# Halved VectorE conversions, two more PSUM banks and later clears in a windowed attention followed by two MLPs

## The chip, the cores and the metric

The kernel runs on one core of a Trainium2 chip. The metric is the time of one execution in microseconds (us) of device time, as the median of several runs. One further execution was recorded by the hardware profiler; all rows below come from it.

## The reference

```python
# attention: B, H, S, D = 4, 8, 576, 64; key j counts for query i where 0 <= i - j < 128
scores = scale * np.matmul(q, k.transpose(0, 1, 3, 2))
scores = np.where(mask, scores + bias[None], -1000000000.0)
attn = softmax(scores);  x = (attn @ v) as 2304 tokens x 512
# first MLP: w_in 512 x 2048, w_out 2048 x 512
h = x @ w_in
g = np.where(h >= 1, h, np.where(h <= -1, 0.0, (h + 1) ** 2 / 4))
x = g @ w_out
# second MLP, weights of the same sizes
h = x @ w_in2
out = (h * np.clip(h + 3.0, 0.0, 6.0) / 6.0) @ w_out2
```

The weights of both MLPs arrive as 64-bit floats. All products are done to nearly 32-bit accuracy, by splitting each operand into a high and a low part.

## The kernel before

The program has three stretches that matter here.

**The opening.** The tokens are cut into units (64 to 256 queries of one batch), and a step is one block of 128 queries (or fewer) of one head of a unit. `Attention.tick` issues one step's stages: `stage_a` multiplies a query block with its keys into a PSUM bank (tile `s`, L418), VectorE adds the table of distances and takes the row's extreme (L448, tiles `p` and `sm`), ScalarE takes the exponential (L452). Two ticks later `stage_b` transposes the result on TensorE (tile `t`, L476 and L477), and ScalarE copies it to `tt`. Three ticks later `stage_c_whole` multiplies it with the values (tile `r`, L514), and at the end of a pair of heads VectorE divides (`rec`, L526 and L527, and `y`, L528). `stage_d_whole` transposes `y` (tile `x` in PSUM, L539), and ScalarE and VectorE write it as a high and a low part into the large tile `x` that feeds the first MLP (L151, L158). The opening runs 37 ticks: the 32 steps of units 0 and 1, and the first steps of unit 2. While `u.unit < 2` the scores take three PSUM banks in turn (`s`, `acc0`, `acc1`) and the transposes two (`t`, `t2`); from unit 2 on they take one each.

**The first block of the first MLP.** `run_block` goes over the 16 pieces f of 128 hidden units for the first 512 tokens. `Mlp.first` makes the first product of piece f, twelve matrix products of 512 columns into one bank (tile `h`, L671). `Mlp1.activate` makes g of it on VectorE, ScalarE and GpSimd: for even f L711, L712, L713, for odd f L704, L705, L706, then the split into a high part (ScalarE, L151) and a low part (GpSimd, L158). Only with L713 or L706 done is the bank free. `Mlp.second` multiplies the g of two pieces earlier into four accumulators (tile `acc`, L724, twelve products). The banks of h are the tags in `mlp1.tags`, here `("h0",)`: one bank, so that the first product of piece f + 1 waits for the activation of piece f. The accumulators are the banks `acc0`, `acc1`, `h1`, `t2`, taken when the first second product is issued, after the first product of piece 2. The remaining ticks of units 2 and 3 are spread through this block.

**The conversion of the first MLP's weights** runs through both. For each piece f, `conv1` makes on ScalarE the shifted magnitude `ma` (L194) and an integer (L198) of the raw words `rawa`, and on GpSimd the sign (L197); `conv2` joins them on VectorE, a shift with or (L205) and an integer addition (L212); `conv3` splits the result into a high part (ScalarE, L151) and a low part (VectorE, L158), tile `wa`. Each handles [128, 1024] elements: the piece's columns of w_in and rows of w_out, 512 each. Pieces 0 to 2 are begun in the opening, at the ticks of `CONV_AT`; the others inside the first block, the conversion of piece f + 2 being finished after the first product of piece f.

`Attention.clear` zeroes at the program's start the half of each of the eight key buffers `kw` that the zero padding needs (L312, VectorE).

A scheduler lays out the instructions of TensorE, VectorE, ScalarE and GpSimd in this part, engine by engine, from the order of the code and its own estimates; each engine then works its list strictly in order. Only SyncE, which issues the transfers, follows the code's own order. After the first block the other blocks of the first MLP (256 and 384 tokens, with the rest of the attention between) and then the second MLP follow, to about 948 us.

Of the kernel before, what the change touches and what calls it, by code (L numbers as in the profile page):

```python
# [9 lines left out]
F32 = mybir.dt.float32  # L10
# [3 lines left out]
I32 = mybir.dt.int32  # L14
# [28 lines left out]
def tile_window_attention_two_mlps(  # L43
# [118 lines left out]
    class Weights:  # L162
# [37 lines left out]
        def conv2(self, f):  # L200


            raw, m = self.raw[f], self.m[f]
            if self.sign_pool:
                nc.vector.scalar_tensor_tensor(out=m.bitcast(U32), in0=m.bitcast(U32), scalar=3, in1=raw[..., 1],  # L205
                                               op0=ALU.logical_shift_left, op1=ALU.bitwise_or)
            else:
                nc.vector.tensor_scalar(out=m.bitcast(U32), in0=m.bitcast(U32), scalar1=3, scalar2=None,
                                        op0=ALU.logical_shift_left)
                nc.vector.scalar_tensor_tensor(out=m.bitcast(U32), in0=raw[..., 1], scalar=0x80000000,  # L210
                                               in1=m.bitcast(U32), op0=ALU.bitwise_and, op1=ALU.bitwise_or)
            nc.vector.tensor_tensor(out=m.bitcast(I32), in0=m.bitcast(I32), in1=raw.bitcast(I32)[..., 0], op=ALU.add)  # L212

        def conv3(self, f):
            del self.raw[f]
            m = self.m.pop(f)
            hl = wpool.tile([P, 2, 2, PIECE], F32R, tag=f"w{f}", name=f"w{self.nm}{f}")
            split_hi("act", hl[:, 0], m)
            split_lo("dve", hl[:, 1], m, hl[:, 0])
            self.hl[f] = hl  # L220

        def conv_part(self, part):
# [54 lines left out]
    class Attention:  # L277
        def __init__(self, raw, proc, work, xs):
            self.raw, self.proc, self.work, self.xs = raw, proc, work, xs
            self.n_load = self.n_prep = self.t = 0  # L280
            self.row, self.low, self.sum, self.late = None, None, None, []
            self.k_owners, self.v_owners = [], []

            self.vts = [raw.tile([P, KCH, 2 * D + 2], F32, tag="vr", name=f"vr{i}", bufs=3) for i in range(3)]

            kr = [raw.tile([P, 2, KMAX], F32, tag="kr", name=f"kw{i}") for i in range(2)]
            qr = [raw.tile([P, 2, UMAX], F32, tag="qr", name=f"qw{i}") for i in range(2)]
            self.kw = [t[:, j] for t in kr for j in range(2)]
            self.kw += [proc.tile([P, KMAX], F32, tag=tag, name=f"kw_{tag}{i}") for tag in ("kh", "kl") for i in range(2)]
            self.qw = [t[:, j] for t in qr for j in range(2)]  # L290
            self.pt = [work.tile([P, 2 * P], F32, tag="p", name=f"p{i}", bufs=LAG_B + 1) for i in range(LAG_B + 1)]
            a = next(h for h in range(H) if plain not in (h, h + 1))
            self.pt.append(dist[:, a:a + 2].bitcast(F32).rearrange("p a b -> p (a b)"))
            free = [h for h in range(a + 2, H) if h != plain]
            self.tc = [dist[:, h:h + 2].bitcast(F32R).rearrange("p a (s q) -> p a s q", s=1)[:, :, 0] for h in free[:4:2]]
            assert len(self.tc) == 2 and all(h + 1 in free for h in free[:4:2])
            self.near, self.takes = zeros[:, :P], zeros[:, P:]
            self.n_p = self.n_tc = 0
# [6 lines left out]
            nc.gpsimd.affine_select(out=self.takes, in_=self.takes, compare_op=ALU.is_ge, fill=0.0,  # L305
                                    base=0, pattern=[[-1, P]], channel_multiplier=1)

        def clear(self):

            for i, k in enumerate(self.kw):  # L310
                a = D * (1 - i % 2)
                nc.vector.memset(k[a:a + D, :], 0.0)  # L312

        def load_whole(self, n):

# [105 lines left out]
        def stage_a(self, n, i):  # L421
# [5 lines left out]
            qo, ko = a - u.q0, ks - u.k0  # L427
            bo = 0 if a >= P else P

            tag = ("s", "acc0", "acc1")[(n * 2 + i) % 3] if u.unit < 2 else "s"  # L430
            ps = psum.tile([P, BANK], F32, tag=tag, name=f"s{n}_{i}")
            u.n_a += 1
            if u.unit == 0:
# [27 lines left out]
        def stage_b(self, n, i):  # L461
# [4 lines left out]
            if i == 0:  # L466
                u.tt = self.work.tile([P, 2, 2 * QB, P], F32 if u.whole else F32R, tag="tt", name=f"tt{n}")
            pt = u.p.pop(i)
            bank = psum.tile([P, BANK], F32, tag=("t", "t2")[(n * 2 + i) % 2] if u.unit < 2 else "t",
                             name=f"t{n}_{i}")  # L470
            ps = bank.rearrange("p (s q) -> p s q", q=P)

# [381 lines left out]
    with ExitStack() as actx:  # L854
# [6 lines left out]
        att = Attention(raw, proc, work, XX)  # L861

        nc.vector.memset(zeros, 0.0)
        att.clear()

        nc.scalar.copy(minus_odd, nc.const_aps.tensor(0.0, [P, 1], F32))
        bank = psum.tile([P, BANK], F32, tag="h1", name="busy")
# [6 lines left out]

        for t in range(unit_steps[0] + unit_steps[1] + LAG_D + 1):
            att.tick()
            if t in LOAD_AT:
                W1.load()
            if t in CONV_AT:
                with att.behind(), att.behind_exp():  # L880
                    W1.conv_part(CONV_AT[t])

        def spread(ticks):

            slots, att0 = 2 * KF, att.t

            def hook(f, after):
                k = 2 * f + after + 1
                W1.load()
                with att.behind(), att.behind_exp():  # L890
                    for part in ((2,) if after else (3, 1)):
                        W1.conv_part(part)
                while att.t < att0 + min(ticks, -(-ticks * k // (slots - 2))):
                    att.tick()

            return hook
# [14 lines left out]

            return hook

        mlp1.tags = ("h0",)
        ticks = unit_steps[2] + unit_steps[3]
        att.make_tables()
        run_block(mlp1, 0, FULL, spread(ticks))
# [434 lines left out]
```

## Time and profile before

| | us |
|---|---|
| median of 3 runs (948.9 to 949.98) | 949.7 |
| the profiled execution | 950.16 |
| its span, first to last instruction | 948.4 |
| TensorE busy (matrix products) | 931.3 |
| VectorE busy | 652.2 |
| ScalarE busy | 535.2 |
| GpSimd busy | 297.1 |

In the profile PE is TensorE's products, PEld its weight loads, DVE VectorE, ACT ScalarE, POOL GpSimd, SP SyncE. A busy time is a union of spans, and the end of a product is modelled, so that a busy PE can still hide short gaps. The duration of an instruction reaches past the start of the next one; how long an engine is taken is the distance from start to start. PEclk is the granted TensorE clock as a share of 2.4 GHz. "[0.52 <-ACT tt L151]" behind a row is idle time ahead of it and the instruction that ended it.

### The profile page before, as it was taken

What the parts mean: (1) busy time and instruction counts of PE and PEld (TensorE: products, weight loads), DVE (VectorE), ACT (ScalarE), POOL (GpSimd) and SP (SyncE); (2) the same over time, 40 slices, a digit from 0 to 9 for tenths busy, and PEclk for the clock granted to TensorE, in tenths of its full rate; (3) what the DMA queues carried; (4) which work ended last, traced back from release to release, by engine and by line L of the source; (5) the groups of instructions that cost most, each with busy time, mean ns of one, the idle gap of its engine ahead of it and who ended that gap; (6) DMA issues with size and microseconds to landing.
All of it is one profiled execution on the core that took longest, in us unless ns stands there. A gap on an engine that the chain in (4) does not pass through costs nothing.

```text
span 948.4 us, 16369 instructions
## 1 busy us (share of the span) xinstructions
PE 931.3 (98%) x5299; PEld 855.1 (90%) x5299; DVE 652.2 (69%) x1706; ACT 535.2 (56%) x1325; POOL 297.1 (31%) x559
## 2 busy tenths in 40 slices
PE   9999999999999999999999999999999999999998
PEld 7777878999999999999999999999998898988887
DVE  5778786786777676766745899958557777644443
ACT  6877876676666666666634886635343334322233
POOL 2133555797668676767720000000000000000000
PEclk9999999999999999999999999999999999999999
DMA  6665512222213222221007862005264644543431
GB/s 195 207 207 193 179 48 73 82 82 84 69 52 88 63 60 63 73 90 48 15 27 250 281 230 90 1 18 172 78 211 157 239 167 151 168 125 117 122 112 66
DMA packets 92644, 112.74 MB, mean 119 GB/s; under 512 B 8720, under 2 KB 70416, under 8 KB 92560
## 3 DMA queue, kind: packets, MB, share of 16 engines
q1 hardware_dynamic: 92560, 111.71, 36.8%
q8 instruction: 42, 0.69, 0.3%
q14 instruction: 42, 0.34, 0.1%
HBM read 87.56 MB, written 24.12 MB: 118 GB/s over the span
## 4 chain that ended last, share of the span: by engine, by line
PE 73%; DVE 7%; ACT 3%; issue 2%; POOL 1%; DMA 1%; SPq 0%; ACTq 0%; POOLq 0%; DVEq 0%
PE acc L777 21%; PE h L671 21%; PE acc L724 13%; PE y L1253 7%; PE x L1253 5%; PE r L562 2%; PE s L418 2%; PE t L477 1%; DVE kl L398 1%; DVE x L158 1%; DVE r L711 1%; DVE r L713 1%; DVE ma L212 1%; DMA x2r<-x2d 1%; ACT r L712 0%
## 5 line engine op out<-in xcount | busy, mean ns | idle before, releaser
L671 PE MATMUL h<-x,wa 128*128 128x384 f32 (+2 forms) x1152 | 222.7, 340 | 4.3 <-DVE r L713 3.1
L777 PE MATMUL acc<-wb,g 128*128 128x512 f32 x861 | 222.2, 393 | 0.0
L724 PE MATMUL acc<-g,wa 128*128 128x384 f32 (+2 forms) x1152 | 222.1, 339 | 0.0
L671 PEld LDWEIGHTS h<-x,wa 128*128 128x128 f32 x1152 | 192.1, 189 | 16.0 <-DVE r L713 6.8
L724 PEld LDWEIGHTS acc<-g,wa 128*128 128x128 f32 x1152 | 190.9, 188 | 5.9
L777 PEld LDWEIGHTS acc<-wb,g 128*128 128x128 f32 x861 | 159.4, 188 | 24.9
L151 ACT CAST g<-r 128x384 fp32r<-128x384 f32 (+2 forms) x192 | 98.2, 511 | 71.0 <-DVE r L1200 37.5
L158 POOL TENSOR_TENSOR g<-r,g 128x384 fp32r<-128x384 f32 (+2 forms) x80 | 87.4, 1093 | 55.9 <-ACT g L151 46.1
L158 DVE TENSOR_TENSOR g<-r,g 128x384 fp32r<-128x384 f32 x112 | 62.3, 556 | 41.9 <-ACT g L151 41.4
L712 ACT ACTIVATE r<-r 128x384 f32<-128x384 f32 (+2 forms) x88 | 45.1, 514 | 70.5 <-DVE r L711 70.3
L495 POOL TENSOR_SCALAR_AFFINE_SELECT tt<-dist 128x256 fp32r<-128x256 f32 (+1 forms) x176 | 77.7, 461 | 16.1 <-DVE dist L490 15.7
L711 DVE TENSOR_SCALAR r<-h 128x384 f32<-128x384 f32 (+2 forms) x88 | 47.5, 540 | 40.5 <-PE h L671 32.0
L671 PE MATMUL h<-x,wb 128*128 128x384 f32 x384 | 72.6, 336 | 0.0
L452 ACT ACTIVATE p<-p,sm 128x128 f32<-128x128 f32 (+2 forms) x134 | 57.4, 430 | 24.8 <-DVE sm L448 24.5
L671 PEld LDWEIGHTS h<-x,wb 128*128 128x128 f32 x384 | 68.2, 188 | 2.6
L713 DVE TENSOR_TENSOR r<-h,r 128x384 f32<-128x384 f32 (+2 forms) x88 | 47.8, 544 | 23.7 <-ACT r L712 21.8
L1198 ACT ACTIVATE r<-u 128x384 f32<-128x384 f32 x32 | 16.8, 525 | 56.2 <-DVE u L1262 56.2
L562 PEld LDWEIGHTS r<-tt,vs 128*128 128x128 f32 x304 | 45.1, 189 | 3.4 <-POOL tt L495 1.3
L400 POOL TENSOR_TENSOR qs<-qr,qs 128x256 fp32r<-128x256 f32 (+2 forms) x64 | 39.0, 610 | 27.1 <-ACT qs L397 15.1
L562 PE MATMUL r<-tt,vs 128*128 128x128 f32 (+3 forms) x304 | 44.8, 262 | 1.6 <-POOL tt L495 0.9
L398 DVE SCALAR_TENSOR_TENSOR kl<-kr,kh 128x256 fp32r<-128x256 f32 (+3 forms) x64 | 39.2, 612 | 0.0
L477 PE MATMUL t<-ident,p 128*128 128x128 f32 x134 | 38.2, 289 | 0.7 <-DVE x L158 0.6
(169 smaller groups left out, 1567.4 us busy)
## 6 DMA issues: line engine op xcount, KB each, us to landing
w<-wd SPq DMA_DIRECT2D x88, 256.0 KB, 2.7
rawa<-w_in SPq DMA_DIRECT2D x16, 512.0 KB, 4.5
rawa<-w_out SPq DMA_DIRECT2D x16, 512.0 KB, 5.6
rawb<-w_in SPq DMA_DIRECT2D x16, 512.0 KB, 4.0
rawb<-w_out SPq DMA_DIRECT2D x16, 512.0 KB, 4.9
wd<-sum SPq DMA_DIRECT2D x32, 256.0 KB, 2.1
wd<-wb SPq DMA_DIRECT2D x24, 256.0 KB, 2.8
out<-o SPq DMA_DIRECT2D x17, 256.0 KB, 2.4
```

The source lines that it names most:

```text
L151: nc.scalar.copy(hi, x)
L158: engines[eng].tensor_tensor(out=lo, in0=x, in1=hi.bitcast(F32), op=ALU.subtract)
L398: nc.vector.scalar_tensor_tensor(out=u.kl[:, :nk], in0=u.kr[:, :nk], scalar=unit, in1=u.kh[:, :nk].bitcast(F32), op0=ALU.mult, op1=ALU.sub ...
L452: self.exp = nc.scalar.activation(out=pt[:, :nk], in_=pt[:, :nk], func=AF.Exp, bias=sm[:, 0:1], scale=-1.0, accum_out=None if u.whole else ...
L495: nc.gpsimd.affine_select(out=u.tt[:, :, s0 + s, :m], in_=both, compare_op=ALU.is_ge, fill=0.0, base=-1 + s, pattern=[[0, 2], [sign, m]], ...
L562: nc.tensor.matmul(u.r[:, qo:qo + nq], u.vs[:, j, c, :, :].rearrange("p a d -> p (a d)"), u.tt[:, part].rearrange("p s q -> p (s q)")[:, s ...
L671: nc.tensor.matmul(ps[:, :n], self.W.w_in(a, c, f), self.x_chunk(x, b, c, n), start=(k == 0), stop=(k == 3 * KC - 1))
L711: nc.vector.tensor_scalar(out=r[:, :n], in0=ps[:, :n], scalar1=-1.0, scalar2=1.0, op0=ALU.max, op1=ALU.min)
L713: self.larger = nc.vector.tensor_tensor(out=r[:, :n], in0=ps[:, :n], in1=r[:, :n], op=ALU.max)
L724: nc.tensor.matmul(acc[i][:, o * n:(o + 1) * n], self.W.w_out(a, f)[:, e * P:(e + 1) * P], g[:, b, :n], start=(first and k == 0 and o == 0 ...
L777: nc.tensor.matmul(acc[t][:, :DM], g[:, b, tg * P:(tg + 1) * P], self.W.w_out(a, f), start=(first and k == 0), stop=(last and k == 2))
L1253: nc.tensor.matmul(ps[:, :N2], w[:, a, c * P:(c + 1) * P], self.x.operand(k, c, b), start=(start and n == 0), stop=(n == 5), skip_group_ch ...
```

## The change

The two `conv2` operations and the low part of `conv3` are issued on VectorE in two halves of 512 columns (`self.sign_pool` is set for the first MLP's weights alone), the shift and the addition of one half before those of the other. The first product of piece 1 takes the bank `t2` instead of `h0`: `mlp1.tags` is `("h0", "t2")` until piece 1, then `("h0",)`. The three banks of scores and the two of transposes stay in use to the end of the opening (`self.open`), so also for the first steps of unit 2. Four of the eight key buffers are cleared at the start, two behind the first tick and two behind the second.

```diff
@@ conv2
             if self.sign_pool:
-                nc.vector.scalar_tensor_tensor(out=m.bitcast(U32), in0=m.bitcast(U32), scalar=3, in1=raw[..., 1],
-                                               op0=ALU.logical_shift_left, op1=ALU.bitwise_or)
+                for k in range(2):
+                    nc.vector.scalar_tensor_tensor(out=m.bitcast(U32)[:, k], in0=m.bitcast(U32)[:, k], scalar=3,
+                                                   in1=raw[:, k, :, 1], op0=ALU.logical_shift_left, op1=ALU.bitwise_or)
+                    nc.vector.tensor_tensor(out=m.bitcast(I32)[:, k], in0=m.bitcast(I32)[:, k],
+                                            in1=raw.bitcast(I32)[:, k, :, 0], op=ALU.add)
+                return
...
@@ conv3
             split_hi("act", hl[:, 0], m)
-            split_lo("dve", hl[:, 1], m, hl[:, 0])
+            if self.sign_pool:
+                for k in range(2):
+                    split_lo("dve", hl[:, 1, k], m[:, k], hl[:, 0, k])
+            else:
+                split_lo("dve", hl[:, 1], m, hl[:, 0])
@@ Attention
+            self.open = True
...
-        def clear(self):
-
-            for i, k in enumerate(self.kw):
+        def clear(self, places):
+
+            for i in places:
                 a = D * (1 - i % 2)
-                nc.vector.memset(k[a:a + D, :], 0.0)
+                nc.vector.memset(self.kw[i][a:a + D, :], 0.0)
...
-            tag = ("s", "acc0", "acc1")[(n * 2 + i) % 3] if u.unit < 2 else "s"
+            tag = ("s", "acc0", "acc1")[(n * 2 + i) % 3] if self.open else "s"
...
-            bank = psum.tile([P, BANK], F32, tag=("t", "t2")[(n * 2 + i) % 2] if u.unit < 2 else "t",
+            bank = psum.tile([P, BANK], F32, tag=("t", "t2")[(n * 2 + i) % 2] if self.open else "t",
@@ the opening and the first block
-        att.clear()
+        att.clear(range(4))
...
             att.tick()
+            if t < 2:
+                with att.behind():
+                    att.clear(range(4 + 2 * t, 6 + 2 * t))
...
                 W1.load()
+                if f == 1:
+                    mlp1.tags = ("h0",)
...
-        mlp1.tags = ("h0",)
+        mlp1.tags = ("h0", "t2")
+        att.open = False
```

TensorE's list where the opening goes over into the first block; `h` is the first product, `wa_469` and then `wa_471` hold piece 0's weights, `wa_616` and then `wa_621` piece 1's, and `x_742`, then `x_750`, is the transpose of the last pair of heads of unit 1. Before:

```order
L514 MATMUL r_724<-vr_105,tt_727 128x65 x2
L476 MATMUL t_0_755<-ident,p_115 128x128
L477 MATMUL t_0_755<-ident,p_115 128x128
L418 MATMUL s_0_764<-kw_kh_110,qw_109 128x192
L476 MATMUL t_0_806<-ident,p_116 128x128
L477 MATMUL t_0_806<-ident,p_116 128x128
L539 MATMUL x_742<-ident,y_704 128x128 x2
L671 MATMUL h<-x,wa_469 128x512 x12
```

And of the changed kernel, in the same place:

```order
L679 MATMUL h<-x,wa_621 128x512 x2
L522 MATMUL r_730<-vr_105,tt_714 128x65 x2
L484 MATMUL t_0_734<-ident,p_114 128x128
L485 MATMUL t_0_734<-ident,p_114 128x128
L679 MATMUL h<-x,wa_621 128x512 x3
L522 MATMUL r_730<-vr_105,tt_733 128x65 x2
L484 MATMUL t_0_763<-ident,p_115 128x128
L485 MATMUL t_0_763<-ident,p_115 128x128
L547 MATMUL x_750<-ident,y_710 128x128 x2
L426 MATMUL s_0_772<-kw_kh_110,qw_109 128x192
L679 MATMUL h<-x,wa_471 128x512 x12
```

Five of the twelve first products of piece 1 now stand ahead of piece 0's, between the opening's last transposes; piece 0's twelve stand ahead of one transpose that they stood behind. Seven products of piece 1 follow piece 0's, and then those of piece 2, ahead of the first second product; before, the twelve of piece 2 stood within the second products of piece 0.

VectorE's list around the division for that last pair of heads (`rec_703`, then `rec_709`, and `y_704`, then `y_710`), with piece 2's `conv2` in it. Before:

```order
L526 TENSOR_SCALAR rec_703<-r_654 128x4
L205 SCALAR_TENSOR_TENSOR ma_667<-ma_667,rawa_449 128x1024
L527 RECIPROCAL rec_703<-rec_703 128x4
L212 ISA ma_667<-rawa_449,ma_667 128x2048
L528 TENSOR_TENSOR y_704<-r_654,rec_703 128x256
```

And of the changed kernel:

```order
L534 TENSOR_SCALAR rec_709<-r_660 128x4
L206 SCALAR_TENSOR_TENSOR ma_673<-ma_673,rawa_451 128x512
L535 RECIPROCAL rec_709<-rec_709 128x4
L206 SCALAR_TENSOR_TENSOR ma_673<-ma_673,rawa_451 128x512
L536 TENSOR_TENSOR y_710<-r_660,rec_709 128x256
L208 ISA ma_673<-rawa_451,ma_673 128x1024 x2
```

Between `rec` and `y` there were a whole shift and a whole addition; now there are the two halves of the shift, and the addition stands behind `y`.

VectorE's list at the program's start, as one piece of the difference:

```order
-L312 MEMSET kw_kh_110 64x384
-L312 MEMSET kw_kh_111 64x384
-L312 MEMSET kw_kl_112 64x384
-L312 MEMSET kw_kl_113 64x384
 L128 TENSOR_SCALAR odd<-odd 128x1
...
+L320 MEMSET kw_kh_110 64x384
+L456 ISA p_115,sm_1_185<-s_1_182,dist 128x256
+L456 ISA sm_1_185 128x1
+L320 MEMSET kw_kl_112 64x384
+L320 MEMSET kw_kh_111 64x384
+L320 MEMSET kw_kl_113 64x384
+L456 ISA p_116,sm_0_197<-s_0_194,dist 128x128
```

One of the four later clears now stands behind the first step's row operation and three behind the second's, ahead of the third's.

## Rows read from the trace of the kernel before

**Rows 1.** Busy time by stage: us, then PE, PEld, DVE, ACT, POOL, clock, DMA.

```profile
0.00:50.49 50.49, 46.39 (x302) 36.91 (x303) 33.62 (x127) 36.11 (x88) 9.76 (x32) 1.00 0.67 200
50.49:62.26 11.77, 10.33 (x50) 8.40 (x49) 7.30 (x17) 7.88 (x15) 3.02 (x4) 0.86 0.91 288
62.26:110.00 47.74, 46.63 (x243) 38.64 (x243) 38.50 (x67) 38.39 (x65) 19.82 (x22) 1.00 0.48 160
110.00:160.00 50.00, 47.79 (x233) 37.77 (x232) 39.17 (x82) 37.03 (x74) 29.63 (x30) 1.00 0.31 94
```

**Rows 2.** PE in order of time: start, us, instruction, count, idle ahead.

```profile
48.68 0.66 PE L514 MATMUL r<-vr,tt 128*128 128x65 f32 x4 [0.52 <-ACT tt L151]
...
50.35 0.38 PE L539 MATMUL x<-ident,y 128*128 128x128 f32 x2
50.49 2.99 PE L671 MATMUL h<-x,wa 128*128 128x512 f32 x12
...
56.77 2.65 PE L671 MATMUL h<-x,wa 128*128 128x512 f32 x6 [1.44 <-DVE r L713]
...
73.19 2.91 PE L671 MATMUL h<-x,wa 128*128 128x512 f32 x12
75.93 0.27 PE L477 MATMUL t<-ident,p 128*128 128x128 f32 x1
```

**Rows 3.** VectorE in order of time, from 47 to 57 us.

```profile
47.20 0.16 DVE L526 TENSOR_SCALAR rec<-r 128x4 f32<-128x4 f32 x1
47.30 1.22 DVE L205 SCALAR_TENSOR_TENSOR ma<-ma,rawa 128x1024 uint32<-128x1024 uint32 x1
48.45 0.17 DVE L527 RECIPROCAL rec<-rec 128x4 f32<-128x4 f32 x1
48.56 1.22 DVE L212 CUSTOM_DVE_ANT_0 ma<-rawa,ma 128x2048 uint16<-128x2048 uint16 x1
49.70 0.42 DVE L528 TENSOR_TENSOR y<-r,rec 128x256 f32<-128x256 f32 x1
...
53.72 0.68 DVE L711 TENSOR_SCALAR r<-h 128x512 f32<-128x512 f32 x1
...
56.02 0.69 DVE L713 TENSOR_TENSOR r<-h,r 128x512 f32<-128x512 f32 x1
```

**Rows 4.** PE's waits, 44 to 160 us: us in total, times, longest.

```profile
PE s L418 <- DVE sm L448: 1.5, 3, 0.6
PE h L671 <- DVE r L713: 1.4, 1, 1.4
```

**Rows 5.** The program's first steps in order of time, PE and VectorE.

```profile
3.94 0.77 PE L418 MATMUL s<-kw,qw 128*128 128x128 f32 x2
...
4.23 0.87 DVE L312 MEMSET kw_kl<- 64x384 f32 x2
...
5.39 0.29 DVE L448 CUSTOM_DVE_ANT_0 p<-s,dist 128x128 f32<-128x128 f32 x1
...
6.37 0.29 DVE L448 CUSTOM_DVE_ANT_0 p<-s,dist 128x128 f32<-128x128 f32 x1
```

**Rows 6.** VectorE, an operation of 256 columns and the start of the next.

```profile
30.51 0.42 DVE L158 TENSOR_TENSOR x<-x,x 128x256 fp32r<-128x256 f32 x1
30.85 0.41 DVE L448 CUSTOM_DVE_ANT_0 p<-s,dist 128x256 f32<-128x256 f32 x1
```

**Rows 7.** GpSimd and VectorE side by side, 121 to 126 us.

```profile
121.54 1.95 POOL L158 TENSOR_TENSOR g<-r,g 128x512 fp32r<-128x512 f32 x1 [0.47 <-ACT g L151]
123.45 2.13 POOL L197 TENSOR_SCALAR rawa<-rawa 128x1024 f32<-128x1024 f32 x1
...
122.51 2.06 DVE L212 CUSTOM_DVE_ANT_0 ma<-rawa,ma 128x2048 uint16<-128x2048 uint16 x1
```

**Rows 8.** The last piece: its conversion's end on VectorE, its first product.

```profile
149.78 1.22 DVE L158 TENSOR_TENSOR wa<-ma,wa 128x1024 fp32r<-128x1024 f32 x1
...
156.52 2.88 PE L671 MATMUL h<-x,wa 128*128 128x512 f32 x12
```

More of the change, by code (lines that the diff above doesn't have):

```diff
@@ L204, in conv2 @@
             if self.sign_pool:
-                nc.vector.scalar_tensor_tensor(out=m.bitcast(U32), in0=m.bitcast(U32), scalar=3, in1=raw[..., 1],
-                                               op0=ALU.logical_shift_left, op1=ALU.bitwise_or)
[L207 to L211, printed above, removed]
+                for k in range(2):
[4 more added lines that the diff above has]
+                return
+            nc.vector.tensor_scalar(out=m.bitcast(U32), in0=m.bitcast(U32), scalar1=3, scalar2=None,
+                                    op0=ALU.logical_shift_left)
+            nc.vector.scalar_tensor_tensor(out=m.bitcast(U32), in0=raw[..., 1], scalar=0x80000000,
+                                           in1=m.bitcast(U32), op0=ALU.bitwise_and, op1=ALU.bitwise_or)
             nc.vector.tensor_tensor(out=m.bitcast(I32), in0=m.bitcast(I32), in1=raw.bitcast(I32)[..., 0], op=ALU.add)
```

## The prediction

> **What bounds the kernel now.** I first read the busy time by stage [rows 1]. From 62 to 160 us TensorE is busy 94.4 of 97.7 us at full clock, while VectorE is busy 77.7 of them (79%) and ScalarE 75.4 (77%): TensorE carries the first block, and the others get in its way for 3.3 us in all. Behind 160 us the change touches nothing but times of arrival, and TensorE's list goes on in the same order, so a us that TensorE is ahead at the end of the first block should be a us at the end of the program. The two stretches ahead of it are looser. In the opening TensorE shows 4.1 us of idle time, and more is hidden in chains from step to step. Between 50.5 and 62.3 us it is idle for 1.44 us and runs at a granted clock of 0.86.
>
> Then I read TensorE in order of time at that seam [rows 2], and who it waited for [rows 4]. The reader is to see one wait: the first product of piece 1 starts at 56.77 us because its only bank is held until piece 0's L713, which starts at 56.02 us [rows 3]. It is the longest wait of the block, and behind it the clock falls to the lower of its two levels (1.2 GHz). A mean of 0.86 over 11.77 us [rows 1] costs 0.14 × 11.77 = 1.65 us.
>
> **The change, part by part.**
>
> *The bank for piece 1.* With its own bank, piece 1's first product follows piece 0's at once: the 1.44 us of waiting go, and with the idle time gone the 1.65 us of lower clock should go too, 3.1 us in all. What is late next is piece 2, which needs piece 0's bank. Ahead of it TensorE has seven products of piece 1: twelve take 75.93 - 73.19 = 2.74 us [rows 2], 0.228 each, so seven take 1.6 us. From the end of piece 0's product the bank needs L711 (0.6 of a row of 0.68, whose tail overlaps the next), two halves of `conv3` that now stand behind it (1.2, below) and L713 (0.7), 2.5 us, with ScalarE's part beneath the halves. So the new wait is between nothing and 0.9 us; four short attention products also lie ahead, and I take 0.5. The term is 3.1 - 0.5 = 2.6 us; its bounds are 0.5 (the clock still falls, and the wait is 0.9) and 3.1.
>
> *The five products moved ahead.* They stand between the transposes of the opening's last steps, where TensorE waited for ScalarE, as for 0.52 us at 48.68 [rows 2]. They are worth 5 × 0.228 = 1.14 us where they fit wholly into waits, and nothing where they push the transposes back. More of that place is idle than the marked wait, so I take 1.0.
>
> *The division ahead of the seam.* Piece 0's product waits for the transpose of `y` (50.35 us), that for `y` (49.70), and that stood behind a whole shift and a whole addition, from 47.30 on [rows 3]. An operation of 1024 columns takes 1.15 us from start to start [rows 3], one of 256 takes 0.34 [rows 6]: 1.06 ns a column and 0.067 us fixed, so a half takes 0.61. Two halves of the shift remain ahead of `y`, so it comes 1.1 us earlier. But TensorE's own steps ahead of that transpose, paced by ScalarE, end barely half a us sooner than they did. Bounds 0 and 1.1; I take 0.7, nearer to the upper since one transpose has left their front.
>
> *The banks for unit 2.* The wait of scores for VectorE's row operation is 1.5 us in three places, the longest 0.6 [rows 4], and only that first place is in the opening. Bounds 0 and 0.6; I take 0.2, because the next steps are paced by ScalarE.
>
> *The clears.* A clear takes 0.44 us (two in 0.87) [rows 5]. The first row operation started at 5.39 us, behind all eight, though its product was finished by 4.71: up to 0.6 us. The third step's row operation, at 6.37, now has three clears ahead: up to 1.3 us lost there. Between these I take a gain of 0.3, as the steps behind it wait for more than VectorE.
>
> The sum ahead of the first second product is 2.6 + 1.0 + 0.7 + 0.2 + 0.3 = 4.8 us.
>
> *The halves inside the first block.* Three more operations for each of 16 pieces at 0.067 us are 3.2 us more of VectorE, some 2.7 of them in the block. VectorE has 20 us of idle time there [rows 1], so the cost isn't felt directly; but TensorE's 3.3 us of waits come where VectorE is late with a row operation or an activation. Halves also change who waits for GpSimd. At 121.54 a GpSimd operation was running, VectorE's addition came at 122.51 and ended at 124.57, 2.06 us for one that takes 1.14 to 1.22 [rows 3, 7]; GpSimd's next came at 123.45 and ended 1.0 us after that addition. They took turns whole. A half that meets a GpSimd operation waits as long as a whole did, and there are twice as many. With some 5 us of such waits beside the 2.7, VectorE's idle time falls from 20 to 13 us, and if waits grow as idle time shrinks, 3.3 become 5.1: 1.8 us. Against that, a row operation now waits 0.6 us instead of 1.15 where the list puts it between halves. I take 1.5 us of loss; bounds are a gain of 3.3 (all waits gone) and a loss of more than the 4.8.
>
> The last piece's weights are ready at about 151 us and used at 156.5 [rows 8]: 5.5 us of slack, just more than the lead. So a lead up to that size needs no faster conversion.
>
> The Trainium skill, "SBUF — State Buffer", Who interferes with whom, says that a VectorE operation with two SBUF inputs and a GpSimd operation that reads SBUF lock each other out for a whole instruction. Rows 7 agree, with 2.06 us against 1.14. By that rule each boundary between halves is a place for GpSimd to step in, which is the slower rival below.
>
> Net, 4.8 - 1.5 = 3.3 us. The profiled execution took 950.16 us (span 948.4 and 1.8 around it), so it would take 946.9; it lies 0.46 above the median of 949.7, on which the forecast is **946.4 us**.
>
> **The rivals.**
>
> *Given back.* VectorE, ScalarE and GpSimd run the first block at nearly their own pace, since each works its list in order, and TensorE, arriving 4.8 us early, waits for them bit by bit until it is where it was. For it: both VectorE and ScalarE are near 80% busy. Against it: the slack of the last piece, and idle time on all three. It gives 949.7 less 0 to 1.9 us.
>
> *Slower, by turns with GpSimd.* Each piece has two long GpSimd operations, L197 and the low part of g. If both come in at a boundary between two halves, VectorE waits 2 × 0.95 us more for a piece (2.06 less about 1.1) [rows 7], 25 us over 13 pieces, with the 2.7 more than its 20 us of idle time: VectorE becomes the bound. It decides when the added waits pass 17 us. The block then grows by 25 + 2.7 - 20 = 7.4 us, less 4.8: 952.3 us. Against it: in most places a whole operation already followed a whole one, so GpSimd could step in there too.
>
> *More is gained.* The smaller operations also take away most of the 3.3 us of later waits instead of adding to them: 4.8 + 2.5 = 7.3 us, 942.4. What speaks for it is 21% of idle time on VectorE; what speaks against it is that the lists mostly put the two halves back to back. The Trainium skill, "Perfetto Trace Analysis", Optimizing Scalar/DVE Operations, says that where these engines aren't saturated but make others wait, breaking up instructions may let work finish sooner. With VectorE at 79% that rule's condition holds here, and by it this case would be the outcome.
>
> **How the numbers follow.** The likeliest case has 0.55, with its own range 943.9 to 947.8 (a net gain of 1.9 to 5.8 us, inside the terms' bounds); given back 0.2; slower by turns 0.13; more is gained 0.12. Differences of 0.2% (1.9 us) are about what a measurement of this kernel can tell from no change. Faster by more than that: 0.55 + 0.12 = 0.67. Within it: 0.2. Slower: 0.13. The range that leaves out 2 in 10 runs from 942.0, which takes in most of the larger gain, to 950.2, which takes in what is given back but not the slower case.
>
> **What would show it.** In the changed profile the first product of piece 0 should start near 49 us instead of 50.49, with five products of piece 1 ahead of it. No wait of 1.4 us should follow it, only one of about 0.5 ahead of piece 2, and the granted clock should stay at 1.00 between 50 and 70 us. The first second product should start near 60 us with 36 first products behind it, instead of 24 at 62.26. A half should take about 0.6 us from start to start. TensorE's waits from there to the last piece should be near 5 us. The prediction is wrong if the clock falls at another place of the seam, if VectorE passes 90% in the first block, or if TensorE's lead at the last piece is far from its lead at the first second product.

## The result, and the profile after

The changed kernel takes 955.71 us (median of 4 runs, 954.2 to 956.2) against 949.84 (948.9 to 950.48). The ratio is 1.0063, with a 95% interval of 1.0048 to 1.0078: it is slower, where the forecast was 946.4 us. The profiled execution has a span of 953.7 us against 948.4.

Busy time by stage after the change, cut at the first product of piece 1 in its new place, at the first second product (62.75 us) and at the first product of block 1 (167.99); columns as in [rows 1]:

```profile
0.00:48.83 48.83, 44.89 (x293) 37.28 (x293) 32.05 (x130) 35.52 (x86) 9.48 (x30) 0.97 0.66 199
48.83:62.75 13.92, 12.50 (x68) 10.06 (x67) 11.18 (x28) 8.53 (x17) 3.42 (x7) 0.99 0.68 219
...
62.75:167.99 105.24, 95.79 (x472) 75.72 (x471) 89.58 (x183) 76.40 (x140) 49.77 (x51) 1.00 0.39 127
```

The stretch of the kernel before from its first second product to the first product of block 1:

```profile
62.26:161.96 99.70, 96.37 (x481) 78.02 (x481) 78.36 (x149) 76.52 (x140) 49.45 (x51) 1.00 0.40 127
```

Two things are to be seen. At its first second product the changed kernel is ahead. It comes 0.49 us later, but behind 36 first products instead of 24, and twelve of them are 2.74 us [rows 2], so the lead is 2.25 us. At block 1's first product it is 167.99 - 161.96 = 6.03 us behind. So 8.3 us were lost between the two, inside the first block. There TensorE is idle for 9.45 us instead of 3.33, and VectorE is busy for 89.58 instead of 78.36. ScalarE and GpSimd do the same work in the same time.

VectorE's conversions from 50 to 170 us, grouped (count, then busy us, mean ns of one, idle time ahead). Before:

```profile
L212 DVE CUSTOM_DVE_ANT_0 ma<-rawa,ma 128x2048 uint16<-128x2048 uint16 x13 | 20.8, 1599 | 0.1
L158 DVE TENSOR_TENSOR wa<-ma,wa 128x1024 fp32r<-128x1024 f32 x14 | 17.3, 1236 | 11.2 <-ACT wa L151 11.1
L205 DVE SCALAR_TENSOR_TENSOR ma<-ma,rawa 128x1024 uint32<-128x1024 uint32 x13 | 17.0, 1305 | 4.8 <-POOL rawa L197 4.7
```

After:

```profile
L208 DVE CUSTOM_DVE_ANT_0 ma<-rawa,ma 128x1024 uint16<-128x1024 uint16 x27 | 28.0, 1060 | 0.0
L158 DVE TENSOR_TENSOR wa<-ma,wa 128x512 fp32r<-128x512 f32 x28 | 22.5, 836 | 0.8 <-ACT wa L151 0.7
L206 DVE SCALAR_TENSOR_TENSOR ma<-ma,rawa 128x512 uint32<-128x512 uint32 x26 | 20.8, 827 | 6.8 <-POOL rawa L197 6.8
```

The same columns are converted in 71.3 us instead of 55.1 (sums of the three groups). Where the 16 us are is seen in the changed kernel in order of time, 87 to 92 us, all engines:

```profile
87.13 1.27 DVE L158 TENSOR_TENSOR wa<-ma,wa 128x512 fp32r<-128x512 f32 x2
...
88.30 1.30 POOL L158 TENSOR_TENSOR g<-r,g 128x512 fp32r<-128x512 f32 x1 [4.85 <-ACT g L151]
...
88.47 3.20 DVE L208 CUSTOM_DVE_ANT_0 ma<-rawa,ma 128x1024 uint16<-128x1024 uint16 x2
...
89.74 1.40 POOL L197 TENSOR_SCALAR rawa<-rawa 128x1024 f32<-128x1024 f32 x1
...
91.59 0.34 DVE L456 CUSTOM_DVE_ANT_0 p<-s,dist 128x192 f32<-128x192 f32 x1
91.76 1.05 ACT L151 CAST wa<-ma 128x1024 fp32r<-128x1024 f32 x1 [1.95 <-DVE ma L208]
...
92.00 0.49 PE L426 MATMUL s<-kw,qw 128*128 128x128 f32 x2 [1.07 <-DVE sm L456]
```

A pair of halves (of the low part) with GpSimd idle for most of it takes 1.27 us (87.13). The pair at 88.47 (of the addition) takes 3.20: it runs beside one GpSimd operation, and a second one begins within it. The row operation behind it comes late, ScalarE waits 1.95 us for the addition, and TensorE 1.07 us for the row operation. It is one of many: of the 81 halves in 50 to 170 us, 18 take over 0.5 us more than the shortest of their kind, none more than 1.14, and each of the 18 overlaps a GpSimd operation that reads. In the kernel before it is 6 of 40 whole operations.

TensorE's waits from 62 to 167 us after the change (us in total, times, longest), as in [rows 4]:

```profile
PE s L426 <- DVE sm L456: 4.0, 6, 1.1
...
PE h L679 <- DVE r L714: 1.7, 2, 1.1
...
PE t L485 <- DVE x L158: 1.6, 2, 0.8
...
PE r L522 <- ACT tt L151: 1.2, 2, 1.0
```

Nearly all of them end with VectorE. None is long; there are simply more of them (15, against 6 in the kernel before from 62 to 162 us).

At the seam, TensorE in order of time after the change (compare [rows 2]):

```profile
45.21 0.66 PE L522 MATMUL r<-vr,tt 128*128 128x65 f32 x4 [1.51 <-ACT tt L151]
...
46.80 1.20 PE L679 MATMUL h<-x,wa 128*128 128x512 f32 x2
47.80 0.95 PE L522 MATMUL r<-vr,tt 128*128 128x65 f32 x4
...
50.83 3.06 PE L679 MATMUL h<-x,wa 128*128 128x512 f32 x12
...
54.53 1.91 PE L679 MATMUL h<-x,wa 128*128 128x512 f32 x7
...
57.41 0.51 PE L679 MATMUL h<-x,wa 128*128 128x512 f32 x1 [0.97 <-DVE r L721]
```

The bank wait of 1.44 us is gone. In its place are 0.97 us ahead of piece 2, and a new wait of 1.51 us for ScalarE at 45.21, behind which the products of 46.80 and 47.80 run slowly: the granted clock is 0.83 from 40 to 50 us, and 1.00 from 50 to 70.

### The profile page after: what moved, and what is told of

It is laid out like the page before. It is cut to its first block, busy times and chain, and to the rows that moved or that the text cites. A ratio compares the mean times of both kernels' runs of the same rounds, so it can differ in the third digit from the quotient of the medians.

```text
span 953.7 us, 16417 instructions
## 1 busy us (share of the span) xinstructions
PE 931.1 (98%) x5299; PEld 855.1 (90%) x5299; DVE 665.6 (70%) x1754; ACT 534.9 (56%) x1325; POOL 297.4 (31%) x559
## 4 chain that ended last, share of the span: by engine, by line
PE 78%; DVE 10%; ACT 5%; issue 3%; POOL 2%; DMA 1%; SPq 0%; ACTq 0%; POOLq 0%; DVEq 0%
PE h L679 22%; PE acc L785 21%; PE acc L732 14%; PE y L1267 7%; PE x L1267 5%; PE s L426 3%; PE r L570 3%; DVE ma L208 2%; PE t L485 2%; DVE ma L206 1%; DVE kl L406 1%; PE r L522 1%; DVE wa L158 1%; DVE r L719 1%; DVE x L158 1%
## 5 line engine op out<-in xcount | busy, mean ns | idle before, releaser
L151 ACT CAST g<-r 128x384 fp32r<-128x384 f32 (+2 forms) x192 | 98.1, 511 | 67.6 <-DVE r L1214 37.6
```

What stands on the lines that cost most here:

```text
L151: nc.scalar.copy(hi, x)
```

## The experiments

Each experiment was timed in five rounds beside the kernel before on its own chip (medians of 949.8 to 950.0 us). Theory A says that the halves cost, because VectorE's two-input operations (both inputs in SBUF) and GpSimd's take turns and more boundaries let GpSimd in. Theory B puts the loss on the seam and the clock's fall there, and theory C on the number of operations and their places in VectorE's list. Besides the times, two measures stand in the table: the conversions' time (sum of the three groups, 50 to 170 us), and the length of the first block, from the first second product to block 1's first product, which starts behind 36 first products, or behind 24 where the table says so.

| kernel | us | conversions, us | first block, us |
|---|---|---|---|
| before | 949.84 | 55.1 | 99.70 (24) |
| after | 955.71 | 71.3 | 105.24 |
| halves_only | 960.77 | 71.4 | 108.37 (24) |
| whole_rest | 947.64 | 57.5 | 98.23 |
| hbank_only | 947.79 | 57.3 | 98.15 |
| open_only | 951.52 | 56.6 | 99.36 (24) |
| hbank_clears | 946.78 | 57.2 | 98.23 |
| before_memset | 947.19 | 55.0 | 98.16 (24) |
| after_memset | 949.02 | 66.6 | 98.98 |
| whole_nolock | 938.08 | 48.9 | 91.95 |
| after_nolock | 936.98 | 54.3 | 92.28 |
| low_whole | 954.13 | 67.6 | 104.85 |
| shift_whole | 949.00 | 62.0 | 100.66 |
| quarters | 959.64 | 84.8 | 108.26 |

**The two parts of the change apart.** whole_rest is the changed kernel with whole conversions:

```diff
-                for k in range(2):
-                    nc.vector.scalar_tensor_tensor(out=m.bitcast(U32)[:, k], in0=m.bitcast(U32)[:, k], scalar=3,
-                                                   in1=raw[:, k, :, 1], op0=ALU.logical_shift_left, op1=ALU.bitwise_or)
+                nc.vector.scalar_tensor_tensor(out=m.bitcast(U32), in0=m.bitcast(U32), scalar=3, in1=raw[..., 1],
+                                               op0=ALU.logical_shift_left, op1=ALU.bitwise_or)
...
-                for k in range(2):
-                    split_lo("dve", hl[:, 1, k], m[:, k], hl[:, 0, k])
+                split_lo("dve", hl[:, 1], m, hl[:, 0])
```

> The changed kernel with the conversions whole again; the banks and the clears stay changed. Theory A (turns): the loss of about 6 us comes from the halves, because VectorE's halves and GpSimd's reading operations take turns whole and there are twice as many places for GpSimd to step in; the 2.2 us of lead that the changed kernel has at the first second product then stays, so 946 to 948.5 us, with VectorE near 80% busy in the first block. Theory B (the seam): the banks or the clears, with the clock that fell earlier (0.83 between 40 and 50 us), start the loss; then 952 to 956 us. Theory C (the lists): any change makes the scheduler lay out other lists, and the loss comes from these; then anything between 950 and 956, with waits for row operations as in the changed kernel.

halves_only is the kernel before with the halves alone (the other side of that diff; banks and clears as before).

> The kernel before with the halves alone. Theory A: slower than the changed kernel or like it, 955 to 958 us, because the lead from the banks is missing; additions of 1024 x 16 bit that take 1.2 us a pair without GpSimd take over 2 us in many pairs, and VectorE is near 90% busy in the first block. Theory B: near 950 us. Theory C: 950 to 956.

Measured: 947.64 us (946.52 to 949.85), ratio 0.9978 (0.9969 to 0.9987), for everything but the halves; 960.77 (960.65 to 963.2), ratio 1.012 (1.0106 to 1.0134), for the halves alone, which is 2.8 us above theory A's bounds. So the halves cost 11 us by themselves and 8.1 on top of the rest. whole_rest in order of time at the seam, TensorE, and its busy time by stage:

```profile
45.03 0.66 PE L516 MATMUL r<-vr,tt 128*128 128x65 f32 x4 [1.13 <-ACT tt L151]
...
50.09 3.03 PE L673 MATMUL h<-x,wa 128*128 128x512 f32 x12
...
54.10 1.67 PE L673 MATMUL h<-x,wa 128*128 128x512 f32 x6
56.23 1.66 PE L673 MATMUL h<-x,wa 128*128 128x512 f32 x6 [0.46 <-DVE r L715]
```

```profile
60.44:158.67 98.23, 94.44 (x468) 75.29 (x467) 78.85 (x146) 75.39 (x138) 52.06 (x50) 1.00 0.42 135
```

The first second product comes at 60.44 us behind 36 first products: a lead over the kernel before of 62.26 - 60.44 + 2.74 = 4.56 us. The first block is 7.0 us shorter than that of the changed kernel. The halves therefore cost 62.75 - 60.44 = 2.3 us at the seam and 7.0 in the block, 9.3 together; the two profiled executions differ by 8.9 us, the medians by 8.1. Some 1.7 of the 2.3 us are the clock's fall between 40 and 50 us, which whole_rest does not have; whether the halves bring it about is not shown.

**The banks apart.** hbank_only gives piece 1's first product its bank and changes nothing else; open_only keeps the second banks of scores and transposes up to the end of the opening and changes nothing else.

```diff
+                if f == 1:
+                    mlp1.tags = ("h0",)
...
-        mlp1.tags = ("h0",)
+        mlp1.tags = ("h0", "t2")
```

> The kernel before with the bank t2 for piece 1's first product alone. By the term of the forecast that belongs to it (wait of 1.44 us gone, a new one of 0.5, the clock's 1.65 us gone or not): 946.5 to 949 us where the lead stays (theory A), 949 to 950 where the other engines give it back in the first block. Theory B has no loss here either unless the clock falls at another place of the seam; it is read from the granted clock between 40 and 70 us.

```diff
-            tag = ("s", "acc0", "acc1")[(n * 2 + i) % 3] if u.unit < 2 else "s"
+            tag = ("s", "acc0", "acc1")[(n * 2 + i) % 3] if self.open else "s"
...
-            bank = psum.tile([P, BANK], F32, tag=("t", "t2")[(n * 2 + i) % 2] if u.unit < 2 else "t",
+            bank = psum.tile([P, BANK], F32, tag=("t", "t2")[(n * 2 + i) % 2] if self.open else "t",
```

> The kernel before with the banks of scores and transposes kept to the end of the opening, alone. Theory A: 949.3 to 950.3 us, as the waits of 0.6 us move within the opening. Theory B: it gathers the opening's short waits into one long wait ahead of the seam, and the clock falls there: 951 to 953 us, with a wait over 1 us for a copy of tt between 43 and 47 us and a granted clock under 0.9 behind it.

Measured: 947.79 us (947.05 to 948.54), ratio 0.9976 (0.9967 to 0.9985), for the h bank; 951.52 (949.77 to 954.05), ratio 1.0019 (1.001 to 1.0028), for the other banks. In hbank_only the clock stays at 1.00 and the lead at the first second product (61.44) is 0.82 + 2.74 = 3.56 us. In open_only a wait of 1.12 us for ScalarE's copies of the transposes stands at 46.34, and the clock falls behind it; it falls again behind the bank wait, which is 1.88 us here (59.73). Its busy time by stage:

```profile
40.00:50.00 10.00, 7.75 (x50) 6.57 (x50) 6.37 (x22) 8.24 (x19) 1.81 (x6) 0.84 0.46 149
50.00:60.00 10.00, 8.10 (x38) 6.84 (x39) 6.89 (x16) 5.76 (x11) 1.45 (x3) 0.82 0.81 264
60.00:70.00 10.00, 10.00 (x46) 8.28 (x46) 6.27 (x14) 7.18 (x14) 4.47 (x5) 0.83 0.35 119
```

That is theory B's effect, and these banks alone lose 1.7 us. (The rows are of an execution of 954.05 us, 2.5 above the median, so they can show more than the median lost.) It explains at most 1.7 us of the changed kernel's loss: there the clock falls once, in 40 to 50 us, for 0.17 × 10 = 1.7 us, while whole_rest, with the same banks and a wait of 1.13 us, keeps its clock and gains.

**Taking GpSimd's reads away.** after_memset (the changed kernel) and before_memset (the kernel before) replace GpSimd's sign operation by a memset of the same places (the weights' signs are left out):

```diff
-                nc.gpsimd.tensor_scalar(out=sign, in0=sign, scalar1=0.0, scalar2=1.0, op0=ALU.mult, op1=ALU.mult)
+                nc.gpsimd.memset(sign, 0.0)
```

> The whole change, with GpSimd's sign operation on the raw weights (2 x 512 columns read and written in SBUF, 1.28 us a piece before, 1.41 us after) replaced by a memset of the same places, which reads nothing. The signs of the weights are left out, so the output is not the reference's. Theory A (the halves cost because each of VectorE's shorter operations can be made to wait for a GpSimd operation that reads SBUF): the conversions' VectorE time in 50 to 170 us falls from 71.3 us to 62 to 66 us, and the kernel stands within 2 us of its own control before_memset, 947 to 951 us. Theory C (the cost is the number of instructions and their places in VectorE's list, which are the same here): conversions stay near 70 us, and the kernel stays 5 to 6 us above its control, 954 to 956 us.

> The kernel before with the same replacement (signs of the weights left out, so the output is not the reference's): the control of after_memset. Theory A: conversions fall from 55.1 us to 50 to 53 us in 50 to 170 us, since the whole operations wait too, but once where the halves wait twice; time 947.5 to 949.8 us. Theory C: nothing of the conversions changes; 949 to 950 us.

Measured: 949.02 us (947.93 to 951.12), ratio 0.9988 (0.9979 to 0.9997), and 947.19 (946.55 to 948.71), ratio 0.9976 (0.9967 to 0.9985). The control is 0.3 us faster than theory A's bounds. The distance between change and control shrinks from 5.9 to 1.8 us. The conversions fell less than forecast (66.6 us, and none in the control); g's low part, which still takes turns, is left. The first blocks, after_memset's and then before_memset's:

```profile
63.39:162.37 98.98, 94.92 (x472) 76.05 (x471) 85.60 (x185) 76.32 (x140) 45.29 (x51) 1.00 0.42 136
60.55:158.71 98.16, 96.03 (x481) 77.95 (x481) 78.46 (x149) 76.94 (x141) 46.21 (x51) 1.00 0.41 134
```

This is the sharpest test of theory C: in after_memset the instructions of TensorE, VectorE and ScalarE are those of the changed kernel in the same order, and so they are in the two kernels before. The change's first block is 105.24 - 98.98 = 6.3 us shorter, the control's 99.70 - 98.16 = 1.5. Set behind the same first products (2.74 us less for the control), the change's block was 8.3 us longer than the control's and is now 3.6 longer, with GpSimd's one operation as the only difference. The clock at the seam has a share in the times too. In the control it holds 1.00 from 50 to 60 us, behind a wait of 1.30 us (56.62) where the kernel before has 1.44 and the lower clock; that alone is some 1.65 of its gain. In after_memset it is 0.77 from 40 to 50 us and 0.89 from 50 to 60, 3.4 us against the change's 1.7. after_memset in order of time, VectorE's and GpSimd's rows:

```profile
81.79 1.29 DVE L208 CUSTOM_DVE_ANT_0 ma<-rawa,ma 128x1024 uint16<-128x1024 uint16 x2
...
86.94 2.39 DVE L208 CUSTOM_DVE_ANT_0 ma<-rawa,ma 128x1024 uint16<-128x1024 uint16 x2
```

```profile
82.19 1.07 POOL L197 MEMSET rawa<- 128x1024 f32 x1 [0.21 <-DMA rawa<-w_out]
86.96 1.82 POOL L158 TENSOR_TENSOR g<-r,g 128x512 fp32r<-128x512 f32 x1 [3.70 <-ACT g L151]
```

A pair of halves of the addition takes 1.29 us with a memset beside it, and 2.39 with g's low part, which reads. A GpSimd operation that only writes doesn't hold VectorE here; one that reads does, by 1.1 us, nearly its own length (1.30 at 88.30 above).

So both of GpSimd's large reading operations were replaced, in the change (after_nolock) and in whole_rest (whole_nolock). Signs and the low parts of g are left out, and GpSimd no longer waits for g's high part.

```diff
-            split_lo(LO[self.g_lo], g[:, 1, :n], r[:, :n], g[:, 0, :n])
+            if LO[self.g_lo] == "pool":
+                nc.gpsimd.memset(g[:, 1, :n].bitcast(F32), 0.0)
+            else:
+                split_lo(LO[self.g_lo], g[:, 1, :n], r[:, :n], g[:, 0, :n])
```

> The whole change with both of GpSimd's operations that read SBUF in the first block, the sign of the raw weights and the low part of g, replaced by a memset of the same places (signs and low parts left out, so the output is not the reference's, and GpSimd does not wait for g's high part any more). What is left of the halves' price is then the fixed cost of 41 more operations, 5.8 us of VectorE's time by the shortest of each kind (54.0 us against 48.2 us). Theory A (turns with GpSimd make most of the loss): the conversions come to 54 to 57 us in 50 to 170 us, and the time lies 1 to 3 us above that of whole_nolock; by the quarters, whose 11.9 us more of fixed cost made the kernel 3.9 us longer, about 2 us. Theory C (number and places of the operations): 6 to 8 us above whole_nolock.

> The control of after_nolock: whole conversions with banks and clears of the change (as whole_rest, 947.64 us) and the same two memsets. Both theories: faster than whole_rest, since the conversions wait for no GpSimd operation (49 to 51 us in place of 57.5 us), 943 to 946 us; it is the distance of after_nolock that tells.

Measured: 936.98 us (936.88 to 937.14), ratio 0.9865 (0.9852 to 0.9879), and 938.08 (937.36 to 939.11), ratio 0.9874 (0.9858 to 0.989). after_nolock's conversions and its first block:

```profile
L208 DVE CUSTOM_DVE_ANT_0 ma<-rawa,ma 128x1024 uint16<-128x1024 uint16 x27 | 18.4, 706 | 0.0
L158 DVE TENSOR_TENSOR wa<-ma,wa 128x512 fp32r<-128x512 f32 x28 | 18.3, 685 | 0.8 <-ACT wa L151 0.8
L206 DVE SCALAR_TENSOR_TENSOR ma<-ma,rawa 128x512 uint32<-128x512 uint32 x26 | 17.6, 703 | 7.2 <-POOL rawa L197 7.2
```

```profile
60.59:152.87 92.28, 92.25 (x472) 76.52 (x471) 74.21 (x183) 75.27 (x140) 31.40 (x50) 1.00 0.45 146
```

whole_nolock's first block:

```profile
61.03:152.98 91.95, 91.42 (x469) 75.94 (x467) 70.80 (x146) 74.79 (x138) 31.11 (x49) 1.00 0.44 143
```

Without GpSimd's two large reading operations (the attention's small ones stay), the halves cost nothing: the first blocks are 92.28 and 91.95 us, and block 1's first product comes at 152.87 and 152.98. The 1.1 us by which the kernel with the halves is faster, where both theories had it slower, arise behind that. TensorE is idle for only 0.03 and 0.5 us of these blocks, so the other engines have more slack here than in the changed kernel, and the lists are not quite those of the changed kernel and whole_rest. Together with after_memset, whose lists are the same, this rules theory C out as the main cause. The fixed cost of the block's 37 more operations (183 less 146) is read here, from VectorE's whole busy time: 74.21 - 70.80 = 3.4 us. The 5.8 us of the expectation, for 41, were too many, since the durations of one kind count tails that overlap the next operation. Both kernels are faster than forecast. The whole conversions lose to the turns too (48.9 us in place of 57.5); how much of the time is the vanished wait for g's high part, and how much lies in the later blocks, where g's low part is a memset as well, was not told apart.

**Which halves.** low_whole has the low part whole again, shift_whole the shift and the addition (the two halves of the diff of whole_rest).

> The whole change, with the low part of the weights (hi subtracted) in one operation of 1024 columns again; shift and add stay in halves. Theory A: the price goes by what the halves add in VectorE's time: by the shortest of each kind 1.9 us of fixed cost and 3.3 us of waiting for the low part, against 3.9 and some 7 for shift and add. So about a third of the 8.1 us comes back: 952.5 to 954 us. Rival (the low part's halves are the ones that hold h's products at the seam, 2.23 us at 54.53 us): the fall of the seam's wait and over half of the loss come back, 948 to 951.5 us.

> The whole change, with shift and add in one operation of 1024 columns each again; the low part stays in halves. Theory A: two thirds of the loss come back, 949.5 to 951.5 us. Rival (the low part's halves are what costs): 952 to 955 us.

Measured: 954.13 us (953.89 to 954.96), ratio 1.0048 (1.0035 to 1.0061), and 949.00 (948.12 to 950.35), ratio 0.9993 (0.9984 to 1.0002). Of the 8.1 us, 1.6 come back with the low part whole and 6.7 with shift and addition whole: the order that theory A had, with both sizes missed (954.13 and 949.00 lie 0.1 and 0.5 outside its bounds). The clock has moved them, here low_whole from 100 to 110 us and shift_whole from 40 to 50:

```profile
100.00:110.00 10.00, 8.15 (x36) 6.65 (x36) 8.92 (x14) 7.05 (x12) 3.85 (x4) 0.86 0.04 12
```

```profile
40.00:50.00 10.00, 8.29 (x59) 6.83 (x58) 7.05 (x23) 7.86 (x19) 2.01 (x7) 1.00 0.55 179
```

The changed kernel has 1.00 and 0.83 there. As an estimate, with 1.7 us for each such fall, the shares are 3.3 and 5.0 us. The rival, which laid the loss on the low part's halves (2.23 us of VectorE at 54.53, ahead of piece 2's products), falls: low_whole has no wait there, and less than half of the loss comes back.

**Quarters.** The same loops over 256 columns:

> The whole change with the conversions in quarters of 256 columns in place of halves of 512. The fixed cost of an operation doubles again: 83 more operations in the first block at about 0.06 us each (1.24 us for a pair of halves against 1.18 us for a whole one) are 5 us of VectorE's time. Theory A: every boundary is a new place for GpSimd to step in, so the waiting grows beside it; conversions 85 to 100 us in 50 to 170 us, time 963 to 975 us. Theory C (a half is put where it blocks a row operation of attention or an h product, and shorter pieces block less): 953 to 958 us.

Measured: 959.64 us (958.2 to 960.86), ratio 1.0103 (1.009 to 1.0116), between the two theories' forecasts. The conversions, grouped:

```profile
L158 DVE TENSOR_TENSOR wa<-ma,wa 128x256 fp32r<-128x256 f32 x56 | 32.8, 639 | 1.1 <-ACT wa L151 0.9
L208 DVE CUSTOM_DVE_ANT_0 ma<-rawa,ma 128x512 uint16<-128x512 uint16 x54 | 27.4, 540 | 0.0
L206 DVE SCALAR_TENSOR_TENSOR ma<-ma,rawa 128x256 uint32<-128x256 uint32 x52 | 24.6, 506 | 2.3 <-POOL rawa L197 2.3
```

The shortest of each kind are 408, 407 and 406 ns, so 162 of them would take 65.9 us. The busy times are unions, which count overlapping tails once, so the means times the counts are set against that: 91.3 us, 25.3 above the shortest. The halves have 73.5 - 54.0 = 19.5 in the same way, and whole_rest's whole operations 9.2. Operations that take over 0.5 us more than the shortest of their kind are 23 of 162, 18 of 81 and 9 of 40. So the waits do grow with the number of boundaries, as theory A has it, but the second doubling added far less than the first. A GpSimd operation can hold VectorE only once, and two boundaries were already enough for most: this is argued from the counts, not shown.

**The best version.** Whole conversions, the h bank and the clears in two lots, without the banks that open_only tried (the two cases in its expectation are on the seam alone):

> Whole conversions, the second bank for h and the clears in two lots; the s and t banks as before (not kept for unit 2). The version that the runs so far point to: the h bank alone gave 947.79 us, and the banks for unit 2 alone lost 1.7 us. Theory A (the clock's fall behind the wait at 45 us comes with the s and t banks): no fall of the clock in 40 to 60 us, 946.5 to 947.8 us. Rival (the clears are worth nothing, or move the seam's wait): 947.8 to 949.5 us.

Measured: 946.78 us (945.84 to 950.03), ratio 0.997 (0.996 to 0.9981), with the clock at 1.00 throughout the seam. It is faster than both kernels; against whole_rest and hbank_only the difference is not certain.

## Why the prediction was wrong

**The seam's banks: right.** The bank for piece 1 and the five products ahead were put at 2.6 + 1.0 = 3.6 us; hbank_only's lead is 3.56: 1.05 of waiting (1.44 less 0.39), the clock's 1.65, and 0.86 left for the products, of which eight stand ahead of piece 0's there. All terms but the halves' own (division, 0.7) make 4.1; whole_rest's lead is 4.56. The wait ahead of piece 2, put at 0.5, is 0.39 in hbank_only (57.09 us) and 0.46 in whole_rest.

**The division: nothing.** y came 1.25 us earlier (48.45 for 49.70), as worked out, but its transpose came at 50.41, and piece 0's product at 50.83, not near 49. TensorE has no marked wait from 45.21 to there: the transpose stood behind TensorE's own list, in part at the lower clock. whole_rest, without this term and with the clock at 1.00, has 50.09.

**The other banks and the clears: sign and place off.** For unit 2's banks 0.2 us were taken; alone they lose 1.7, with a wait for ScalarE at 46.34 us and the lower clock behind it. The clears moved the first row operation from 5.39 to 4.77 us and the third from 6.37 to 7.39, as expected; hbank_clears and hbank_only differ by 1.0 us, within their spreads.

**The lead: not all of it stays.** Even without halves some is given back in the first block: whole_rest's lead of 4.56 us is 161.96 - 158.67 = 3.29 at block 1's first product, hbank_only's 3.56 is 2.37. The sum had nothing for that; the rival "given back" had it in full.

**The clock: at another place.** It holds 1.00 from 50 to 70 us, as said, and falls from 40 to 50 instead: 1.7 us, as much as the place removed was worth. A fall at another place of the seam was one of the prediction's signs of being wrong.

**The halves: the failed step.** The prediction took "1.5 us of loss" for the halves inside the first block; they cost 7.0 us there, and 2.3 at the seam, where the term had nothing (some 1.7 of these are the clock). Its first half was right in kind and too low: 2.7 us of fixed cost (3.4 measured) and "some 5 us of such waits" come to 7.7 of VectorE's time, and 89.58 - 78.85 = 10.7 were added against whole_rest, so 7.3 of waits. The failure is the next step, "if waits grow as idle time shrinks, 3.3 become 5.1". It spread the added time evenly over VectorE's idle time. It comes in lumps of about 1 us instead, two of them at the pair at 88.47, and a lump delays the row operation or the activation right behind it (there TensorE's 1.07 at 92.00). TensorE's idle time became 9.45, not 5.1. VectorE was at 85% in the block, below the 90% named as a sign, and did not have to be the bound. The sign that came is the lead: 2.25 us ahead at the first second product, 6.03 behind at block 1's first product. (Two sums of the prediction are off: 20 less 7.7 is 12.3 us of idle time, not 13, which gives 5.4 for 5.1; and the 7.4 of the slower rival is reached with 24.7, not with the 25 printed. Neither changes the outcome.)

The rival "slower, by turns with GpSimd" is what happened; it had a chance of 0.13, and its 952.3 us assumed that VectorE becomes the bound, which it did not. Against it the prediction had said that GpSimd could step in between whole operations too. It can; but a half that ends while a GpSimd operation waits leaves its own second half standing for that operation, which a whole conversion does not (88.47). The Trainium skill, "SBUF — State Buffer", Who interferes with whom, says that two-input VectorE operations contend with GpSimd instructions that read SBUF and not with those that only write. The runs agree on both counts: 2.39 us beside g's low part, 1.29 beside a memset. The Trainium skill, "Perfetto Trace Analysis", Optimizing Scalar/DVE Operations, says that breaking up instructions may let work finish sooner where these engines are not saturated but make others wait. No run shows that gain from the halves: with GpSimd's large reads away the first block is 92.28 us against 91.95, and with them the halves cost 8.1 us.

**What stays open.** How the 7.0 us of the block divide between the fixed cost, delayed row operations, activations and weights is not told apart; nor why the clock fell behind 1.12 us of waiting in open_only and not behind 1.13 in whole_rest. One execution of each kernel was recorded, so it is not known either whether the clock falls in all executions of a kernel.

## What to carry to other kernels

Before an operation of VectorE with two SBUF inputs is cut into pieces, look for GpSimd operations that read SBUF beside it, and price a wait of up to one whole GpSimd operation for each that can now step in (here at most 1.14 us, at 18 of 81 halves). Price such a delay at the instruction that stands behind it, not as a share of the engine's idle time: TensorE was idle for 6 us more (9.45 against 3.33) beside an engine that was 85% busy. Where several edits come together, time each alone: here the bank alone gains 2.0 us, and that gain is hidden behind another edit's loss of 8.

## What the hardware showed unexpectedly

A memset on GpSimd runs beside VectorE's two-input operations without delaying them (82.19 us in after_memset). Replacing the reading operations shortens the kernel with whole conversions by 9.6 us (947.64 to 938.08), GpSimd's wait for g's high part among it. And waits of TensorE that are nearly alike are followed by the lower clock in one kernel and not in another: 1.12 us at 46.34 in open_only (0.84 and 0.82 in the two stretches of 10 us) and 1.13 at 45.03 in whole_rest (1.00); 1.44 at 56.77 in the kernel before (0.86) and 1.30 at 56.62 in before_memset (1.00).
